# A fused attention and feed-forward kernel on one core: attention of batches 2 and 3 planned half a tile further ahead, pieces of the last tiles regrouped, and the fallback program moved within the instruction stream

## The chip, the core and the metric

The kernel runs on one core of a Trainium2 chip. The core has five engines with instruction streams of their own: PE (TensorE, matmuls), DVE (VectorE), ACT (ScalarE), POOL (GpSimd) and SP (SyncE, which here issues DMAs). [...] The metric is the device time of one execution in microseconds, lower is better.

## The reference

Attention over 4 batches, 8 heads, 768 positions and a head size of 64, where some heads ("retrieval" heads, flagged in an input; three of eight here) see all earlier positions, and the others see only the first `n_sink` = 4 positions and the last `window` = 64. Its output, as 3072 rows of 512, goes through a feed-forward layer with the activation h - tanh(h).

```python
def _attn_ref(q, k, v, is_retrieval, n_sink, window):
    scores = scale * np.matmul(q, k.transpose(0, 1, 3, 2))
    causal = rel >= 0
    stream_keep = causal & (is_sink | in_win)
    mask = np.where(retr[0, :, 0, 0, None, None], full_mask, stream_mask)
    scores = np.where(mask[None, :, :, :], scores, -1000000000.0)
    scores = scores - np.max(scores, axis=-1, keepdims=True)
    a = np.exp(scores)
    a = a / (np.sum(a, axis=-1, keepdims=True) + 1e-09)
    return np.matmul(a, v).astype(np.float32)

def _moe_ref(x, w_in, w_out):
    h = x @ w_in            # 512 -> 2048
    g = h - np.tanh(h)
    return (g @ w_out).astype(np.float32)   # 2048 -> 512
```

## The kernel before

**Tiles.** The 3072 rows are cut into 12 tiles of 256, three to a batch (tile t belongs to batch t // 3). For each tile there is attention (4 pairs of heads), a first layer of 8 units and a second layer. Tiles 3 to 11 use heads sorted by rank, so that the flagged heads come first; this is right for up to four flagged heads. If there are more, a second complete program, the redo program, computes everything again without that assumption. A count of flagged heads is loaded into a register of each engine near the end, and each engine compares it with 4 and branches.

**The operations.** For a pair of heads of a tile: SP or POOL loads q, k and v (L609), POOL gathers them by rank into fp16 (L654, L690) and builds helper tiles `vf` and `kc` (L709 to L729, L669, L679), SP transposes q and k with two DMA transposes a tile (L573, tile `QK`), PE computes scores (L1082), ACT the exponentials (L1095, tiles `pt` for pairs with flagged heads and `ptn` for the others), DVE multiplies with a mask (L1145, L1111, L1117; L1135 for tile 2), PE multiplies with the values (L1174), DVE divides by the sum (reciprocal L1194, scaling L1206 into `x16t`), and SP transposes the finished tile (L1238, tile `xT`). First layer: PE (L1298, 8 matmuls of 256 columns for a unit), ACT tanh (L1310), DVE the gate (L1317, tile `gt`, or `gu` for tile 2). Second layer: for tiles up to 7, 16 matmuls of 512 columns for each half of the tile (L1356), ACT evacuation (L1330), a store by SP.

**Tiles 8 to 11 have a cheaper second layer.** It uses seven products of half size in place of eight (the function `piece`, L1478, 8 matmuls of 256 columns each). For it DVE makes four sums of parts of w_out once for all tiles (`combine`, L1396: five steps in four parts each, called T below), and four sums of parts of the tile's gates for each tile (`sums`, L1446, called S, written into `m4`, in `SH` parts each). The results are put together by ACT (`take`, L1513), DVE (`fold`, L1532) and POOL (`add`, L1543) and stored by `send` (L1563). For tiles 8 to 10, `step(t, i)` runs beside unit i of the next tile's first layer and does what the table `STEPS` lists for i: numbers are pieces, letters are takes, folds and stores. For tile 11, `finale` does all seven pieces in one go.

**The order.** Every operation is recorded with an engine, a cost and what it reads and writes; the record's place is its priority. The class `Plan` then lays all of them out in time: at each step the engine that can start first takes its ready operation of the lowest priority number, with PSUM banks, buffers and DMA queues accounted for. The order that comes out is the order in which each engine's instructions are issued. The places in the record come from slots: one slot for each first-layer unit. `point(h)` is the slot of half tile h. The attention of batches 2 and 3 is cut into six visits a batch, each with three score units; visit i of batch b is recorded at half tile 6b - LEAD + i, its gather `GA` slots ahead, its loads `LD` slots ahead. `CUT1` does the like for the tiles of batch 1. `TWHEN` says over which slots the T sums are recorded (the first sixteen parts from the first entry to the second, the last four at the third); a part also reads a mark that the first gate of tile `TG` writes, if that gate is recorded before it.

**The end.** The last instructions of the main program are the last folds and stores. The last store is issued by ACT, the one before by SP. Then each engine compares and branches. The redo program stands directly behind that branch, so an execution that does not need it takes the branch, to a block of closing waits (SP waits there for all landings) and on to the common end with two barriers. A hint about this branch is given to each engine at the start of the program:

```python
tc.mark_branch_hint_location("redo", hint="LikelyTaken", engines=[...])
...
with tc.If(many[0] > NGEN, label="redo"):
    program(False)
```

Names and lines of the prediction's steps: scores L1082, exponentials L1095, masks L1145 and L1111, values L1174, first layer L1298, gates L1317, T sums L1396, S sums L1446, pieces L1478, folds L1532, stores L1563, transposes L573 (`QK`) and L1238 (`xT`), value loads L609 (`rawv`), the branch and the closing waits L1889, the hint and the common end L1921.

Of the kernel before, what the change touches and what calls it, by code (L numbers as in the profile page):

```python
# [255 lines left out]
def kernel(  # L256
# [14 lines left out]
    ALU = mybir.AluOpType  # L271
# [3 lines left out]
    DM = out.shape[1]  # L275
# [3 lines left out]
    NTT = NT // TT  # L279
# [8 lines left out]
    NGEN = H // 2  # L288
# [19 lines left out]
    Engine = mybir.EngineType  # L308
# [28 lines left out]
    CM = DM // 2  # L337
# [10 lines left out]
    many = []  # L348
# [6 lines left out]
    CASTS = (('ACT', 'DVE'), ('ACT', 'ACT'))  # L355
    CUT = (-4.5, -4.0, 5.25, 9.5)
    GATE = {3: (1, 0), 4: (1, 0)}
    CUT1 = (-8.0, -7.0, 3.0, 14.5)
    FLEX = 2
    ST = 8  # L360
    TQ = 4
    TG = 4
    SH = 2
    TWHEN = ((6, 0), (8, 0), (9, 1))
    STEPS = {1: (1, 4, "a"), 3: (2, 6, "e"), 5: (5, "b"), 7: (3, 7, "f")}
    TRI = ()
    SPLIT = 1 << 30
    LEAD = 3
    QUART = 7
    LD = 14  # L370
    GA = 10
    FROM = 3
    BR = 1
    AFTER = {3: 2}
# [12 lines left out]
    def program(first):  # L387
# [1004 lines left out]
        def combine(k, h, fn, a, b, w=lambda: ()):  # L1392
# [5 lines left out]
                ),  # L1398
                r=every + [("T", x, h) for x in range(1, 5) if x != k] + [("at", TG)],
                w=[("T", k, h), *w()], port=True,  # L1400
# [27 lines left out]
        def summed(k):  # L1428
            return [("S", k, h) for h in range(SH)]

        def sums(t):
# [4 lines left out]
            for k, fn, a, b, r in (  # L1436
# [4 lines left out]
            ):  # L1441
                for h in range(SH):
                    cs = slice(h * NC // SH, (h + 1) * NC // SH)
                    op(
                        "DVE", 90 + 690 // SH,
                        lambda k=k, fn=fn, a=a, b=b, cs=cs: getattr(nc.vector, fn)(  # L1446
                            out=S4[k][:, cs, :], in0=a()[:, cs, :], in1=b()[:, cs, :]
                        ),
                        r=g_[h * NFU // SH : (h + 1) * NFU // SH] + [("S", x, h) for x in r],
                        w=[("S", k, h)] + ([("m4", x) for x in range(HP)] if t == ST else []),  # L1450
# [5 lines left out]
        def piece(t, p, beside=None):  # L1456

            gt, ig, tag = gts[t]
            A = lambda i, f: lambda c: gt()[:, 2 * c + f, i * 128 : (i + 1) * 128]
            W = lambda f, m: lambda c: W_(f, m)[:, c, :]  # L1460
            T = lambda k: lambda c: T_(k)[:, c, :]
            S = lambda k: lambda c: S4[k - 1][:, c, :]
            lhs, rhs, r = {
                1: (A(0, 0), W(0, 0), []), 2: (A(0, 1), W(1, 0), []),
                3: (S(4), W(1, 1), summed(3)), 4: (A(1, 1), T(4), both(4)),
                5: (S(1), T(1), summed(0) + both(1)),
                6: (S(2), T(2), summed(1) + both(2)),
                7: (S(3), T(3), summed(2) + both(3)),
            }[p]
# [83 lines left out]
        def send(t, x, lo, hi, dst, ring="SP"):  # L1553

            ot, io = unit(t, x)
            how = "(r two) m -> r two m" if mixed(t) else "(two r) m -> r two m"
            rows = out[t * TT : (t + 1) * TT, :].rearrange(how, two=2)

            def go():
                src = ot()[:, lo:hi]  # L1560
                if len(dst(rows).shape) == 3:
                    src = src.rearrange("p (a b) -> p a b", b=dst(rows).shape[2])
                engs[ring].dma_start(out=dst(rows), in_=src)  # L1563

            dma(
                ring, 420, go, 128, (hi - lo) * 0.18, r=at_(t, x, lo, hi) + [("ot", io)], lag=(500, 800),
            )
# [3 lines left out]

        def step(t, i):

            for what in STEPS.get(i, ()):
                if what == "a":
                    take(t, 1, "A", 0, DM)
                elif what == "e":
                    fold(t, 2, "A", 0, "E", 0)
                elif what == "b":
                    take(t, 5, "A", 0, CM)  # L1580
                    add(t, "POOL", "tensor_sub", ("E", CM), ("A", 0), ("E", CM))
                    add(t, "POOL", "tensor_add", ("A", CM), ("A", 0), ("A", CM))
                elif what == "f":
                    fold(t, 3, "E", CM, "F", 0)
                    send(t, "F", 0, DM, columns(1))
                    add(t, "POOL", "tensor_sub", ("E", CM), ("A", CM), ("F", CM))
                    send(t, "E", 0, DM, columns(0))
                else:
                    piece(t, what, {4: 1, 6: 2, 7: 3}.get(what))

        def finale(t):

            piece(t, 1)
            take(t, 1, "A", 0, CM)
            piece(t, 4)
            take(t, 4, "F", 0, CM)
            piece(t, 2)
            fold(t, 2, "A", 0, "E", 0, CM)
            send(t, "E", 0, CM, lambda rows: rows[:, 0, 0:CM])
            piece(t, 6)  # L1600
            fold(t, 6, "A", 0, "E", CM, CM)
            add(t, "POOL", "tensor_add", ("F", 0), ("E", CM), ("F", 0))
            piece(t, 5)
            fold(t, 5, "E", CM, "A", CM, CM, 1.0, ALU.subtract)
            piece(t, 7)
            fold(t, 7, "F", 0, "F", 0, CM, -1.0)
            send(t, "F", 0, CM, lambda rows: rows[:, 1, 0:CM])
            fold(t, 7, "A", CM, "F", CM, CM)
            send(t, "F", CM, DM, lambda rows: rows[:, 1, CM:DM])
            piece(t, 3)  # L1610
            fold(t, 3, "A", CM, "E", CM, CM)
            send(t, "E", CM, DM, lambda rows: rows[:, 0, CM:DM], "ACT")
# [181 lines left out]
        if first and fast:  # L1794
            spread_over([by_rank], BR, BR)
            qs = quads()
            spread_over(qs[: 4 * TQ], slot_of[TWHEN[0]], slot_of[TWHEN[1]])
            spread_over(qs[4 * TQ :], slot_of[TWHEN[2]], slot_of[TWHEN[2]])
        spread_over(att_pairs(1) + [lambda: scale_v(1, SV)], 0, 0)
# [7 lines left out]
        for b in range(FLEX, NTT // NG) if first and fast else ():  # L1807
# [36 lines left out]
        for s, what in enumerate(slots):  # L1844
            if first and fast and s == point(2 * NG * FLEX - LEAD - 1):
                P.split = len(P.ops)
            fs = plan.get(s, [])
            mid = (len(fs) + 1) // 2
            for i, x in enumerate(what):
# [8 lines left out]
                else:  # L1858
                    t, ts, f0, f1, c0, c1 = x[1:]
# [3 lines left out]
        last = NTT - 1  # L1863
        if first and fast:

            def count():
                many.append(
                    nc.values_load(
                        count_i[0:1, 0:1], min_val=0, max_val=H,
                        skip_runtime_bounds_check_because="it counts the flags of H heads",  # L1870
                    )
                )
                tc.mark_branch_hint_location("redo", hint="LikelyTaken", engines=[Engine.Activation, Engine.PE, Engine.DVE, Engine.SP, Engine.Pool])

            op("SP", 500, count, r=["count", ("gt", gts[last][1], NFU - 1)])
        if quick(last):
            sums(last)
            finale(last)
        else:
            O_group(last, 0, 0, NFB)  # L1880
            O_group(last, 1, 0, NFB, 0, half, "DVE", "SP")
            O_group(last, 1, 0, NFB, half, DM, "ACT", "ACT")

        with tc.manual_schedule():
            P.run()

    program(True)
    if fast:
        with tc.If(many[0] > NGEN, label="redo"):  # L1889
            program(False)  # L1890


# [33 lines left out]
```

## Time and profile before

| | us |
|---|---|
| median of 3 runs | 230.2 |
| lowest and highest | 229.33, 230.72 |
| the profiled execution | 230.94 |
| its span in the profile | 229.2 |

The profile shows one execution. Its page lists busy time by engine, a picture of the span in 40 slices, the DMA queues, the chain of work that ended last, and the costliest groups of instructions; further views give groups by stage, one line's or one tile's instructions, and a timeline. A row of a timeline has start, length, engine, line, operation, tiles written and read, and how many such instructions are merged in it; "SPq" or "ACTq" is work of an engine's sequencer, such as issuing a DMA or branching. A matmul's shown length overlaps the next one's, so the distance between starts is what a matmul costs PE.

### The profile page before, as it was taken

The page shows a single profiled execution, that of the slowest core. Times are in us where ns is not written, and L with a number is a line of the kernel's source. Part 1 is how long each engine was busy: PE and PEld are TensorE (multiplying, and loading weights), DVE is VectorE, ACT ScalarE, POOL GpSimd, SP SyncE. Part 2 cuts the span into 40 slices and gives each one's busy share as a digit, 9 for nine tenths or more (in the row PEclk, how much of TensorE's full clock was granted, in tenths as well). Part 3 has the DMA queues.
Part 4 walks back from the last instruction along what each step waited for, and adds up shares of the span by engine and source line. Part 5 has one row for each costly group of instructions (what it writes and reads, how often), then busy time and mean ns, then how long its engine had stood idle before and what let it go on. Part 6 is the DMA issues. An engine that isn't in the chain of part 4 may idle for free.

```text
span 229.2 us, 6385 instructions
## 1 busy us (share of the span) xinstructions
PE 219.0 (96%) x2415; PEld 166.6 (73%) x2415; DVE 165.8 (72%) x401; ACT 141.1 (62%) x219; POOL 109.0 (48%) x241
## 2 busy tenths in 40 slices
PE   7979999999999999999999999999999999999990
PEld 7556687788986666765765867675868889898880
DVE  5787957865684955989886575476889599684891
ACT  3828839977466847746466657655883766732610
POOL 8989344775641918777465829290000021042020
PEclk9999999999999999999999999999999999999999
DMA  5999999999999999999999999936031042022032
GB/s 157 150 188 203 202 191 223 215 181 238 194 153 212 193 179 236 230 252 172 257 201 227 205 227 185 235 94 141 3 92 49 0 49 93 3 47 94 0 114 80
DMA packets 103877, 35.33 MB, mean 154 GB/s; under 512 B 90658, under 2 KB 101922, under 8 KB 103842
## 3 DMA queue, kind: packets, MB, share of 16 engines
q1 hardware_dynamic: 86544, 27.14, 57.8%
q0 software_dynamic: 17152, 7.60, 25.5%
q8 instruction: 20, 0.33, 0.6%
q10 hardware_dynamic: 146, 0.13, 0.2%
q14 instruction: 15, 0.12, 0.2%
HBM read 27.26 MB, written 6.29 MB: 146 GB/s over the span
## 4 chain that ended last, share of the span: by engine, by line
PE 71%; DMA 11%; POOL 6%; DVE 3%; ACT 3%; SPq 2%; issue 2%; POOLq 0%; DVEq 0%
PE banks L1298 29%; PE banks L1356 21%; PE banks L1478 10%; DMA win<-in_moe_w_in_dram 7%; PE banks L1174 6%; PE banks L1082 5%; DMA rawqk<-in_k_dram 2%; DMA QK<-t 2%; SPq L573 2%; POOL v L507 2%; ACT pt L1095 1%; POOL win L621 1%; POOL t L654 1%; POOL t16p L540 1%; DVE ot L1532 1%
## 5 line engine op out<-in xcount | busy, mean ns | idle before, releaser
L1298 PE MATMUL banks<-xT,win 128*128 128x256 f16 x768 | 94.8, 273 | 0.8 <-DVE gt L1317 0.6
L1298 PEld LDWEIGHTS <-win 128*128 128x128 f16 x768 | 73.0, 98 | 16.4 <-issue 1.6
L1310 ACT ACTIVATE th<-banks 128x512 f32<-128x512 f32 x96 | 57.2, 604 | 39.4 <-PE banks L1298 38.3
L1317 DVE SCALAR_TENSOR_TENSOR gt<-th,banks 128x512 f16<-128x512 f32 x88 | 59.7, 682 | 18.6 <-ACT th L1310 17.8
L1095 ACT ACTIVATE pt<-banks 128x768 f16<-128x768 f32 (+1 forms) x60 | 53.0, 922 | 10.5 <-PE banks L1082 10.2
L1356 PE MATMUL banks<-wout,gt 128*128 128x512 f16 (+1 forms) x288 | 57.1, 332 | 0.0
L654 POOL CAST t<-rawqk 128x256 f16 x72 | 29.2, 451 | 31.9 <-DMA rawqk<-in_k_dram 31.9
L1356 PEld LDWEIGHTS <-gt 128*128 128x128 f16 x288 | 25.8, 98 | 13.8 <-issue 1.0
L1543 POOL TENSOR_TENSOR ot<-gu,ot 128x256 f32<-128x256 f32 x6 | 4.5, 749 | 57.2 <-ACT gu L1513 42.5
L1206 DVE TENSOR_TENSOR x16t<-banks,rinv 128x128 f32 (+1 forms) x80 | 22.5, 286 | 1.1
L1082 PE MATMUL banks<-QK 64*128 64x128 f16 (+1 forms) x364 | 21.0, 238 | 1.0 <-DMA QK<-t 0.8
L690 POOL CAST v<-rawv 128x128 f16 x72 | 21.9, 349 | 0.0
L1082 PEld LDWEIGHTS <-QK 64*128 64x128 f16 x364 | 12.8, 94 | 10.0 <-issue 7.3
L1095 ACT ACTIVATE ptn<-banks 128x1024 f16<-128x1024 f32 (+1 forms) x18 | 17.1, 953 | 3.6 <-DVE x16t L1206 2.4
L1174 PEld LDWEIGHTS <-pt 128*128 128x128 f16 x420 | 15.9, 97 | 4.4 <-DVE pt L1145 0.9
L1174 PE MATMUL banks<-v,pt 128*128 128x65 f16 x220 | 16.5, 193 | 0.4 <-DVE xT L970 0.3
L1145 DVE TENSOR_TENSOR pt<-pt,m4r 128x1024 f16<-128x1024 f16 (+1 forms) x18 | 12.5, 696 | 5.1 <-ACT pt L1095 5.0
L1330 ACT ACTIVATE ot<-banks 128x512 f32<-128x512 f32 (+1 forms) x20 | 10.5, 524 | 8.5 <-PE banks L1356 7.2
L1117 DVE TENSOR_TENSOR ptn<-ptn,mS 128x1024 f16<-128x1024 f16 x12 | 9.6, 804 | 7.6 <-ACT ptn L1095 7.4
L1478 PEld LDWEIGHTS <-m 128*128 128x128 f16 x128 | 12.2, 98 | 1.7 <-issue 0.2
L1174 PE MATMUL banks<-vf,pt 128*128 128x65 f16 x200 | 13.1, 193 | 0.2 <-ACT pt L1095 0.2
L1194 DVE RECIPROCAL rinv<-banks 128x4 f32<-128x4 f32 x48 | 8.2, 175 | 5.5 <-PE banks L1174 5.0
(105 smaller groups left out, 239.9 us busy)
## 6 DMA issues: line engine op xcount, KB each, us to landing
rawqk<-in_q_dram SPq DMA_DIRECT2D x18, 256.0 KB, 4.2
rawqk<-in_k_dram SPq DMA_DIRECT2D x18, 256.0 KB, 4.6
out_dram<-ot SPq DMA_DIRECT2D x18, 256.0 KB, 2.6
rawv<-in_v_dram SPq DMA_DIRECT2D x16, 256.0 KB, 5.1
win<-in_moe_w_in_dram POOLq DMA_DIRECT2D x4, 512.0 KB, 11.7
wout<-in_moe_w_out_dram POOLq DMA_DIRECT2D x4, 512.0 KB, 13.3
out_dram<-ot SPq DMA_DIRECT2D x11, 128.0 KB, 4.0
v<-in_v_dram POOLq DMA_DIRECT2D x6, 128.0 KB, 9.5
```

Source lines behind the costliest of these rows:

```text
L654: nc.gpsimd.tensor_copy(out=c5()[:, :, :, s_ : s_ + 1, :], in_=r5()[:, :, :, at, :])
L690: nc.gpsimd.tensor_copy(out=v1s[b]()[:, g * NB : g * NB + NB, RANK[s_] : RANK[s_] + 1, 0:D], in_=rv()[:, :, at, :],)
L1082: nc.tensor.matmul(out=sc()[:, hh, o : o + nb * 128], lhsT=lhsT, rhs=QK[p_, hp, q_0 : q_0 + nb * 128], start=not added, stop=not added or ...
L1095: lambda pt=pt, sc=sc, gi=gi, wid=wid: nc.scalar.activation(out=pt()[:, :, 512 * gi : 512 * gi + wid], in_=sc()[:, :, 0:wid], func=AF.Exp, ...
L1145: nc.vector.tensor_mul(out=pv, in0=pv, in1=m)
L1174: nc.tensor.matmul(out=av()[:, i, hh, :], lhsT=pt()[:, hh, co : co + 128], rhs=vv, start=(jb == first_jb), stop=(jb == qb),)
L1206: nc.vector.tensor_mul(out=xt()[:, :, at, :], in0=av()[:, :, hh : hh + 1, 0:D], in1=rinv()[:, :, hh : hh + 1].unsqueeze(3).to_broadcast([1 ...
L1298: nc.tensor.matmul(out=ph()[:, j, :], lhsT=w_in_t[fb // 4][:, cb, f0 : f0 + 128], rhs=x, start=(cb == 0), stop=(cb == HP - 1),)
L1310: lambda: nc.scalar.activation(out=th()[:], in_=ph()[:], func=AF.Tanh, scale=1.0 / XS),
L1317: lambda: nc.vector.scalar_tensor_tensor(out=gt()[:, u * FU : (u + 1) * FU, :], in0=th()[:], scalar=-XS, in1=ph()[:], op0=ALU.mult, op1=AL ...
L1356: nc.tensor.matmul(out=po()[:, c0:c1], lhsT=gt()[:, f, ts * 128 : ts * 128 + 128], rhs=w_out_t[:, f, c0:c1], start=(f == 0), stop=(f == NF ...
L1478: nc.tensor.matmul(out=po()[:, at : at + CM], lhsT=lhs(c), rhs=rhs(c), start=c == 0, stop=c == NC - 1,)
```

## The change

It has five parts.

1. Attention of batches 2 and 3: `LEAD` from 3 to 4, so each visit is recorded one half tile earlier; `GA` from 10 to 7, so the gather comes 7 slots ahead of the visit instead of 10. `CUT1` shifts the attention of tiles 4 and 5 in the record.
2. T sums: the first sixteen parts are recorded from tile 4 on instead of tile 6 (`TWHEN`), the last four two slots later in tile 9; the mark that they read is tile 5's (`TG`).
3. Pieces: tiles 8 and 9 start their pieces at unit 2 instead of 1, tile 10 keeps the old table under the name `STEPL`. Each S sum is one instruction over the whole tile instead of two over its halves (`SH`), which makes 16 instructions of DVE fewer.
4. The old `finale` is kept as `finale_b`, and `FIN = 0` selects it; a new `finale` with another order of pieces stands in the file and is not called. The second-last store goes to ACT (`ENDS`).
5. The hint is gone, and the `If` gets `preferred_fallthrough_block=False`.

```diff
-    CUT1 = (-8.0, -7.0, 3.0, 14.5)
+    CUT1 = (-8.0, -5.0, 4.0, 14.5)
...
-    TG = 4
-    SH = 2
-    TWHEN = ((6, 0), (8, 0), (9, 1))
-    STEPS = {1: (1, 4, "a"), 3: (2, 6, "e"), 5: (5, "b"), 7: (3, 7, "f")}
+    TG = 5
+    SH = 1
+    TWHEN = ((4, 0), (8, 0), (9, 3))
+    STEPS = {2:(1, 4, "a"),4:( 2, 6, "e"), 5: (5, "b"), 7:(3, 7, "f")}
+    STEPL = {1: (1, 4, "a"), 3: (2, 6, "e"), 5: (5, "b"), 7: (3, 7, "f")}
...
-    LEAD = 3
+    LEAD = 4
+    FIN = 0
+    ENDS = "ACT"
...
-    GA = 10
+    GA = 7
...
-            for what in STEPS.get(i, ()):
+            for what in (STEPS if t < NTT - 2 else STEPL).get(i, ()):
...
         def finale(t):
...
+        def finale_b(t):
...
             fold(t, 7, "F", 0, "F", 0, CM, -1.0)
             send(t, "F", 0, CM, lambda rows: rows[:, 1, 0:CM])
             fold(t, 7, "A", CM, "F", CM, CM)
-            send(t, "F", CM, DM, lambda rows: rows[:, 1, CM:DM])
+            send(t, "F", CM, DM, lambda rows: rows[:, 1, CM:DM], ENDS)
             piece(t, 3)
             fold(t, 3, "A", CM, "E", CM, CM)
             send(t, "E", CM, DM, lambda rows: rows[:, 0, CM:DM], "ACT")
...
-                tc.mark_branch_hint_location("redo", hint="LikelyTaken", engines=[...])
...
-            finale(last)
+            (finale if FIN else finale_b)(last)
...
-        with tc.If(many[0] > NGEN, label="redo"):
+        with tc.If(many[0] > NGEN, label="redo", preferred_fallthrough_block=False):
             program(False)
```

In the built instruction streams the blocks stand in this order: before, main program, redo program, closing waits, common end; after, main program, closing waits, redo program, common end. So in both there is one jump over the redo program on each engine: before, it is the compare ahead of the closing waits; after, it is an unconditional branch behind them. On SP 117 instructions lie between branch and target in both, on the other engines between 114 (POOL) and some 4,870 (PE).

More of the change, by code (lines that the diff above doesn't have):

```diff
@@ L1596, in finale @@
             take(t, 4, "F", 0, CM)
+            piece(t, 6)
+            fold(t, 6, "A", 0, "E", CM, CM)
+            add(t, "POOL", "tensor_add", ("F", 0), ("E", CM), ("F", 0))
+            piece(t, 7)
+            fold(t, 7, "F", 0, "F", 0, CM, -1.0)
+            send(t, "F", 0, CM, lambda rows: rows[:, 1, 0:CM])
+            piece(t, 5)
+            fold(t, 5, "E", CM, "A", CM, CM, 1.0, ALU.subtract)
+            fold(t, 7, "A", CM, "F", CM, CM)
+            send(t, "F", CM, DM, lambda rows: rows[:, 1, CM:DM])
+            piece(t, 3)
+            fold(t, 3, "A", CM, "E", CM, CM)
+            send(t, "E", CM, DM, lambda rows: rows[:, 0, CM:DM], ENDS)
+            piece(t, 2)
+            fold(t, 2, "A", 0, "E", 0, CM)
+            send(t, "E", 0, CM, lambda rows: rows[:, 0, 0:CM], "ACT")
+        def finale_b(t):
+            piece(t, 1)
+            take(t, 1, "A", 0, CM)
+            piece(t, 4)
+            take(t, 4, "F", 0, CM)
             piece(t, 2)
@@ L1872, in count @@
                 )
-                tc.mark_branch_hint_location("redo", hint="LikelyTaken", engines=[Engine.Activation, Engine.PE, Engine.DVE, Engine.SP, Engine.Pool])
             op("SP", 500, count, r=["count", ("gt", gts[last][1], NFU - 1)])
```

## Prediction

> **What bounds the kernel now.** I read the page first, then the busy time by stage, then PE's own timeline where it is not full, then everything behind PE's last matmul.
>
> ```profile
> PE 219.0 (96%) x2415; PEld 166.6 (73%) x2415; DVE 165.8 (72%) x401; ACT 141.1 (62%) x219; POOL 109.0 (48%) x241
> ...
> PE 71%; DMA 11%; POOL 6%; DVE 3%; ACT 3%; SPq 2%; issue 2%; POOLq 0%; DVEq 0%
> ```
>
> PE is busy 96% of the span of 229.2 us and carries 71% of the chain that ended last. The table by stage (columns: stage, its length, then busy us of PE, PEld, DVE, ACT, POOL) tells where anything is left:
>
> ```profile
> 90.00:103.00 13.00, 13.00 (x140) 9.49 (x137) 11.45 (x29) 8.12 (x12) 10.43 (x25) 1.00 1.07 230
> 103.00:109.00 6.00, 5.80 (x61) 3.31 (x60) 5.75 (x15) 3.90 (x6) 4.54 (x11) 1.00 1.00 176
> 109.00:120.00 11.00, 11.00 (x105) 7.54 (x104) 9.49 (x24) 6.50 (x10) 6.82 (x18) 1.00 1.10 229
> 120.00:222.00 102.00, 102.00 (x1090) 79.56 (x1088) 75.25 (x169) 61.52 (x94) 29.60 (x70) 1.00 0.49 104
> ```
>
> From 120 to 222 us PE is busy 102.00 of 102.00 us at a granted clock of 1.00: an order that does the same matmuls cannot finish that stage sooner. The one hole behind 90 us lies in 103 to 109, where DVE is busy 5.75 of 6.00 us. PE's timeline there:
>
> ```profile
> 106.50 0.36 PE L1174 MATMUL banks<-v,pt 128*128 128x65 f16 x6
> 106.69 0.60 PE L1298 MATMUL banks<-xT,win 128*128 128x256 f16 x4
> 107.39 0.35 PE L1174 MATMUL banks<-v,ptn 128*128 128x65 f16 x6
> 107.58 0.60 PE L1298 MATMUL banks<-xT,win 128*128 128x256 f16 x4
> 108.28 0.35 PE L1174 MATMUL banks<-v,pt 128*128 128x65 f16 x6
> ```
>
> Two rows of the chain of waits give what a matmul occupies when nothing is late: 0.216 us with 512 columns, 0.109 with 256.
>
> ```profile
> 144.75 1.73 PE banks L1356 x8
> ...
> 210.31 6.99 PE banks L1298 x64
> ```
>
> Four of 256 columns take 0.44 us, so PE should go on at 107.13 and 108.02 but goes on at 107.39 and 108.28: two waits of 0.26 us, and one of 0.15 before 106.50, where eight of 512 columns from 104.61 should have ended at 106.34. Together 0.67 us. The chain says what was late:
>
> ```profile
> 105.00 0.55 DVE t16p L1396
> 105.54 0.89 DVE pt L1145
> 106.44 0.89 DVE ptn L1111
> 107.33 0.43 DVE t16p L1396
> 107.75 0.48 DVE pt L1145
> ```
>
> The masks of tile 6 queue on DVE behind the weight sums of line 1396. Everything after PE's last matmul is the other place:
>
> ```profile
> 223.88 0.42 DVE L1532 SCALAR_TENSOR_TENSOR ot<-banks,gu 128x256 f32<-128x256 f32 x1
> 224.00 0.51 SPq L1563 DMA_DIRECT2D out_dram<-ot  x1
> 224.34 0.39 ACTq L1563 DMA_DIRECT2D out_dram<-ot  x1
> ```
>
> ```profile
> L1889 SPq EVENT_SEMAPHORE  x8: 17/17/17, 225.1 to 227.5; - x8
> ...
> L1889 PEldq COMPARE_BRANCH  x1: 2091/2091/2091, 222.2 to 222.2; - x1
> ...
> L1889 SPq COMPARE_BRANCH  x1: 73/73/73, 224.6 to 224.6; - x1
> ```
>
> ```profile
> L1921 SPq EVENT_SEMAPHORE  x14: 17/28/28, 227.6 to 229.1; - x14
> ...
> L1921 SPq BRANCH_PREFETCH_HINT  x1: 56/56/56, 0.8 to 0.8; - x1
> ```
>
> The last fold ends at 224.30, ScalarE issues the last store at 224.34, SP has waited for its landing by 227.5, and closing waits and barriers take to 229.2. SP's branch over the redo program (224.6) lies ahead of that wait, so it is hidden under 2.9 us of landing.
>
> **The change part by part.**
>
> *Attention ahead (LEAD 4, GA 7, CUT1, TWHEN, TG).* The same 2,415 matmuls stand in the built order, the first 1,025 (to 90.8 us) in the same places. The first score visit of tile 6 moves from place 1,157 (104.0 us) to 1,115 (97.8 us). Loads and gathers hardly move: GpSimd's list differs by one memset, SP's by small swaps. Of the weight sums, five now stand on DVE ahead of the mask at 50.31, the other eleven of the first sixteen behind tile 5's first gate, that is behind 109; so none is left in 94 to 109, where they took some 6 us.
>
> ```profile
> L1396 DVE TENSOR_TENSOR t<-wout x4: 389/536/826, 94.2 to 98.1; 128x512 f16<-128x512 f16 x4
> ```
>
> ```profile
> 50.31 1.39 DVE L1135 SCALAR_TENSOR_TENSOR pt<-m,pt 128x512 f16<-128x512 f16 x2 [1.72 <-ACT pt L1095]
> ```
>
> ```profile
> 53.43 0.25 PE L1174 MATMUL banks<-vf,pt 128*128 128x65 f16 x3
> ```
>
> Five at 0.39 to 0.54 us take 2.0 to 2.7 us from 48.6 us, of which 1.72 is idle now: the mask starts 0.3 to 1.0 late and ends by 52.7 at the latest, before PE wants it at 53.43. Cost nothing; without that cover, up to 1.0. Queued behind are a reciprocal and two scalings whose bank PE wants later.
>
> The 0.67 us go if tile 6's masks now find DVE free. The built order has 8 + 4 matmuls of the layers between the scores and their first use (0.44 + 0.86 + 0.87 = 2.2 us) where it had 1.7. Full gain -0.67. What is late next is tile 7:
>
> ```profile
> 99.18 1.93 SPq L609 DMA_DIRECT2D rawv<-in_v_dram  x1
> 101.66 2.06 SPq L1238 DMA_TRANSPOSE xT<-x16t  x1
> 103.83 2.62 SPq L573 DMA_TRANSPOSE QK<-t  x2
> ```
>
> ```profile
> 109.35 0.59 PE L1356 MATMUL banks<-wout,gt 128*128 128x512 f16 x2
> ```
>
> Its score visit takes the place that PE now reaches at 109.35, about 108.6 with the waits gone. Its operands come from the two transposes, the second issued at 105.1; from issue to landing they need
>
> ```profile
> DMA to landing us min/median/max: 3.2/3.3/5.0
> ```
>
> that is 108.3 or later. In the new order SP issues xT of tile 5 before that value load; if xT's scalings come about a us sooner with the weight sums gone, all lands about 107.5. While SP waits for them, the value load and both transposes queue behind it. New waits: between 0 and 1.5 us (the longest landing, 5.0, gives 110.1); I take +0.25, near the low end, for the median is the likelier landing and the next visit that needs new operands, tile 8's, stands 160 places further on. The other DMAs that move past each other on SP are stores and loads that no one awaits within a us.
>
> *Last tile's first layer (STEPL, later STEPS) and whole-tile sums (SH 1).* The first layer of tile 11 moves from places 2,291 to 2,354 in one run to 2,239 to 2,342 between the pieces of tile 10. PE has no hole there to fill, so 0. Whole sums wait for a whole tile: four of at most 2 x 0.42 us follow the last gate, which now ends about 217.3 instead of
>
> ```profile
> 218.03 0.68 DVE L1317 SCALAR_TENSOR_TENSOR gt<-th,banks 128x512 f16<-128x512 f32 x1
> ...
> 221.10 0.41 DVE L1446 TENSOR_TENSOR m<-gt,m 128x512 f16<-128x512 f16 x1
> ```
>
> 217.3 + 3.4 + one fold of 0.68 = 221.4, against 222.81 less 0.7, when the last piece starts. Hidden, by 0.7 us; without the earlier layer it would cost about 0.7.
>
> *Second-last store by ScalarE (ENDS; FIN 0 keeps the old finale under a new name).* It is ready at 223.88 and can be issued at 223.91 instead of 224.00; only the last store queues behind its 0.39 us and is ready at 224.30. Between -0.1 and +0.4; taken with the landing, next.
>
> *Redo program behind the end, no hint.* The hint at 0.8 us leaves every engine: -0.06. In the built order the redo program now stands behind the closing waits but ahead of the common end. So each engine falls through its compare and, after its closing waits, takes a jump over the redo program without a hint. For SP this jump comes after the last landing, with nothing over it. Its price: SP's branch starts at 224.6 and the next wait at 225.1, 0.5 us for a jump over 117 instructions, and the new one spans 117 too: +0.5. Bounds 0.07 (its own row) and 2.1 (PE's row, much of which is waiting for its matmuls); I take 0.5, the same engine and distance. [...] PE, VectorE and ScalarE jump from about 224.4 to 225.0; even 2.1 us later they stand before the barrier that SP reaches at 228.4.
>
> ```profile
> q8 instruction: 1, 0.02, 1.4%
> ```
>
> ```profile
> q10 hardware_dynamic: 18, 0.02, 3.9%
> ```
>
> The first row is the DMA table of 224.0 to 229.2: one code packet of 16 KB takes 1.4% of 16 engines' 5.2 us, 1.16 us on one engine. The second is that of 226.0 to 227.2: the last store's queue moves 18 of its 144 packets there, about one engine's share of two late rows, after all others are done by 226. If code no longer lies ahead of them the landing comes 1.0 sooner; if two packets do, up to 0.6 later. I take -0.2.
>
> *Sum*, on the span: -0.06 - 0.67 + 0.25 + 0.5 - 0.2 = -0.18, 229.0. The profiled execution took 230.94 around a span of 229.2 (1.74 outside) and stands 0.74 above the median of 230.2, so I forecast 230.0.
>
> **The rivals.**
>
> A, slower: the jump finds its code missing on SP. [...] Here: SP's unhinted jump at about 227 costs PE's 2.1 us in place of 0.5, or more: 230.0 + 1.6 = 231.6. It decides the time as soon as SP's jump exceeds about 1.9. For it: no hint is left, and code packets do run at the end. Against: 117 instructions are few and SP's present jump of that length takes 0.5. Chance 0.17.
>
> B, slower: tile 7's transposes land after 5.0 us, SP being held by xT of tile 5 (+1.5 instead of 0.25), and the eleven sums, now behind 109, queue one of 0.5 us ahead of a mask: 231.7. For it: four sums stand in 109 to 120 now, eleven then. Against: DVE has 1.5 of 11 us free there, and gates can wait where masks cannot. Chance 0.10.
>
> C, faster: the final stores come clear of code packets (-1.0 instead of -0.2) with no new wait: 229.0. For it: the 18 late packets. Against: PE's unhinted jump fetches code at about the same time. Chance 0.23.
>
> D, the change does not do what it says: the stall only moves, and the jump is dearer by what the branch was: 230.0 + 0.5 = 230.5. This stays with the forecast's side, chance 0.12; the forecast itself 0.38.
>
> **How the numbers follow.** A change within 0.5% (1.15 us) is about what a measurement of this kernel can tell from none. Forecast and D: same, 0.50. C: faster, 0.23. A and B: slower, 0.27. The forecast's own range is 229.1 to 230.9; with A's fetch of up to 2 us and C's gain it becomes 228.6 to 231.9.
>
> **What would show it.** Right: no hole in PE between 103 and 112; tile 6's scores near 97.8; the last fold near 223.6; no hint row; SP's branch row after its last landing wait, and about 0.5 us to its next row. Wrong: PE waiting for the QK transposes near 108.5, holes behind 120, a branch row on SP of 2 us, or a last store that lands 2 us after issue instead of 3.1. Two or more such waits that I did not list would put it beyond the range.

## The result and the profile after

The changed kernel takes 231.84 us (median of 11 runs, 230.78 to 232.20) against 230.66 us before (median of 11, 229.33 to 231.87): a ratio of 1.0052, 95% interval 1.0030 to 1.0073. The forecast was 230.0 us and no change. The time lies outside the forecast's own range, 229.1 to 230.9, and just inside the wider one, 228.6 to 231.9, whose upper end came from rival A. The change costs about 1.2 us, more than the measurement's uncertainty.

The profiled execution took 232.18 us around a span of 230.0 us. From its page, the engine totals and the chain that ended last:

```profile
PE 218.7 (95%) x2415; PEld 167.1 (73%) x2415; DVE 161.4 (70%) x385; ACT 141.2 (61%) x219; POOL 109.4 (48%) x241
...
PE 86%; DMA 3%; ACT 3%; POOL 2%; DVE 2%; issue 1%; POOLq 0%
```

PE carries still more of the chain (86%, before 71%). The table by stage (stage, length, then busy us of PE, PEld, DVE, ACT, POOL, then granted clock):

```profile
90.00:97.00 7.00, 6.47 (x80) 4.73 (x78) 4.92 (x11) 5.69 (x9) 4.18 (x8) 1.00 1.08 211
97.00:103.00 6.00, 5.98 (x73) 4.36 (x73) 4.80 (x15) 3.37 (x6) 5.64 (x16) 1.00 0.99 190
103.00:109.00 6.00, 6.00 (x52) 3.91 (x50) 4.01 (x11) 3.00 (x6) 2.81 (x7) 1.00 1.10 226
109.00:120.00 11.00, 11.00 (x118) 7.49 (x113) 10.12 (x25) 8.20 (x12) 7.12 (x18) 1.00 1.02 206
120.00:222.00 102.00, 102.00 (x1073) 79.69 (x1071) 72.42 (x154) 59.29 (x92) 30.85 (x71) 1.00 0.44 102
```

The hole between 103 and 109 us is gone (6.00 of 6.00, before 5.80), and VectorE is busy 4.01 us there instead of 5.75. But 90 to 97 us, which was full (7.00), now has a hole (6.47). The timeline there (start, length, engine, line, operation; in brackets the idle time before and what ended it):

```profile
94.62 0.69 DVE L1120 TENSOR_TENSOR ptn<-ptn,mS 128x1024 f16<-128x1024 f16 x1 [0.94 <-ACT ptn L1098]
...
95.45 1.03 PE L1359 MATMUL banks<-wout,gt 128*128 128x512 f16 x4
95.65 0.60 ACT L1313 ACTIVATE th<-banks 128x512 f32<-128x512 f32 x1 [0.57 <-PE banks L1301]
...
96.28 0.69 DVE L1320 SCALAR_TENSOR_TENSOR gt<-th,banks 128x512 f16<-128x512 f32 x1 [0.28 <-ACT th L1313]
...
97.02 0.19 PE L1177 MATMUL banks<-vf,ptn 128*128 128x65 f16 x1 [0.54 <-DVE gt L1320]
```

Four matmuls of 512 columns from 95.45 are through at 96.31 (4 x 0.216 us, what one took in the profile before: 8 in 1.73 us), and PE goes on at 97.02: 0.71 us. The mask of line 1120 was done at 95.31, so it is not the mask. PE waits for a gate of line 1320 (96.28 to 96.97), which itself comes behind an activation.

The end, first the timeline behind the last matmul:

```profile
222.58 0.89 DVE L1535 SCALAR_TENSOR_TENSOR ot<-banks,gu 128x256 f32<-128x256 f32 x2
222.69 0.34 SPq L1566 DMA_DIRECT2D out_dram<-ot  x1
223.02 0.87 ACTq L1566 DMA_DIRECT2D out_dram<-ot  x2
```

then the rows of line 1914 (the branch and the closing waits) and of line 1946 (the end; after the count: shortest/median/longest ns, then first and last start):

```profile
L1914 SPq EVENT_SEMAPHORE  x8: 17/17/17, 223.2 to 227.8; - x8
...
L1914 PEldq COMPARE_BRANCH  x2: 95/2256/4418, 221.4 to 223.2; - x2
...
L1914 SPq COMPARE_BRANCH  x2: 38/46/53, 223.1 to 227.9; - x2
L1914 ACTq COMPARE_BRANCH  x2: 38/46/53, 223.9 to 224.1; - x2
```

```profile
L1946 SPq EVENT_SEMAPHORE  x14: 17/28/28, 228.4 to 230.0; - x14
...
L1946 DVEq DRAIN  x2: 10/36/61, 226.9 to 229.5; - x2
L1946 ACTq DRAIN  x2: 8/38/67, 227.2 to 229.5; - x2
L1946 PEldq DRAIN  x2: 8/40/73, 227.7 to 229.5; - x2
```

and the DMA queues between 224.1 and 227.7 us (packets, MB, share of 16 engines' time):

```profile
q10 hardware_dynamic: 244, 0.22, 19.4%
q8 instruction: 1, 0.02, 3.7%
q14 instruction: 3, 0.02, 2.6%
```

How these read: the last fold ends at 223.47, 0.83 us sooner than in the profile before (224.30), and ScalarE issues the last store at about 223.50 (the second of the two from 223.02). Before, SP had seen the last landing by 227.5, some 3.1 us after that issue at 224.34; now it sees it by 227.8, some 4.3 us after the issue. SP's jump then goes out at 227.9 and its next wait starts at 228.4: 0.5 us, with nothing beside it. PE's jump takes 4.4 us (223.2 to 227.6), and ScalarE's and VectorE's next instructions come at 227.2 and 226.9, about 3 us after their jumps. All three stand before the barrier in time. But the one 16 KB code packet of queue q8 has taken 3.7% of 16 x 3.6 us, or 2.1 us; before, it took 1.16 us. The trace doesn't name the engine whose code a packet carries. Queue q8 is taken for PE's here, since its 21 packets of 16 KB are 0.34 of the 0.48 MB of code in the span of this profile and 4,830 of the 6,367 instructions are PE's matmuls and weight loads; q14, with 18 packets of 8 KB, is taken for the other engines'.

The span grows by 0.83 us between the two profiles, from 229.21 to 230.03. PE reaches its matmul number 1,000 (counted from 0) 0.84 us sooner, at 88.60 instead of 89.44 us. From there to the start of its last matmul it takes 134.13 us in both. Behind that start it takes 7.30 us instead of 5.63. So the earlier last fold isn't the work of the closed hole: it comes from the stretch ahead of matmul 1,000, which holds the same matmuls in the same order. Other runs of the kernel before's order reach that matmul anywhere from 87.5 to 89.4 us.

Two things outside these rows. The time outside the span is 2.10 us on average in the changed kernel's 11 runs, against 1.74 us in the profiled execution of before; later runs of before average 1.75. So about 0.35 of the 1.2 us lies there. And this profile has a slow stretch of TensorE's clock at 16 to 20 us (0.61 granted). One of six later profiles with this order has such a stretch too (0.69), and in all seven PE reaches matmul 1,000 at 87.8 to 88.6 us, so it isn't what costs.

### The profile page after: what moved, and what is told of

Its sections match the earlier page's. It is cut to its first block, busy times and chain, and to the rows that moved or that the text cites. A ratio compares the mean times of both kernels' runs of the same rounds, so it can differ in the third digit from the quotient of the medians.

```text
span 230.0 us, 6367 instructions
## 1 busy us (share of the span) xinstructions
PE 218.7 (95%) x2415; PEld 167.1 (73%) x2415; DVE 161.4 (70%) x385; ACT 141.2 (61%) x219; POOL 109.4 (48%) x241
## 4 chain that ended last, share of the span: by engine, by line
PE 86%; DMA 3%; ACT 3%; POOL 2%; DVE 2%; issue 1%; POOLq 0%
PE banks L1301 35%; PE banks L1359 24%; PE banks L1481 11%; PE banks L1085 7%; PE banks L1177 7%; DMA t16p<-in_k_dram 3%; ACT pt L1098 1%; PE banks L1074 1%; POOL v L510 1%; ACT QK L971 1%; ACT th L1313 1%; DVE gt L1320 1%; PE banks L990 0%; POOL A L758 0%; PE banks L1259 0%
## 5 line engine op out<-in xcount | busy, mean ns | idle before, releaser
L1301 PE MATMUL banks<-xT,win 128*128 128x256 f16 x768 | 97.4, 274 | 0.5 <-DVE gt L1320 0.5
L657 POOL CAST t<-rawqk 128x256 f16 x72 | 31.6, 486 | 36.4 <-DMA rawqk<-in_k_dram 33.4
L1546 POOL TENSOR_TENSOR ot<-gu,ot 128x256 f32<-128x256 f32 x6 | 5.3, 883 | 54.7 <-ACT gu L1516 45.9
L693 POOL CAST v<-rawv 128x128 f16 x72 | 18.8, 307 | 0.0
L1120 DVE TENSOR_TENSOR ptn<-ptn,mS 128x1024 f16<-128x1024 f16 x12 | 8.8, 736 | 9.1 <-ACT ptn L1098 9.0
```

The costliest lines, as they stand in the source:

```text
L657: nc.gpsimd.tensor_copy(out=c5()[:, :, :, s_ : s_ + 1, :], in_=r5()[:, :, :, at, :])
L693: nc.gpsimd.tensor_copy(out=v1s[b]()[:, g * NB : g * NB + NB, RANK[s_] : RANK[s_] + 1, 0:D], in_=rv()[:, :, at, :],)
L1301: nc.tensor.matmul(out=ph()[:, j, :], lhsT=w_in_t[fb // 4][:, cb, f0 : f0 + 128], rhs=x, start=(cb == 0), stop=(cb == HP - 1),)
```

## The experiments

Twelve kernels ran. Names that begin with a_ start from the changed kernel, with b_ from the kernel before. All ratios are to the kernel before, run beside them, with the 95% interval. A first table, since all the sections draw on it. "Order": attention as before or new. "Redo": ahead of the closing waits (old) or behind them (new). PE from 1,000 is the time from the start of PE's matmul number 1,000, counted from 0, to that of its last, in the profiled run; there is one profile of each kernel. The next columns are us after the start of the last matmul: PE's last 16 KB code packet that starts between 1 us ahead of that matmul and 3 us behind it (start + length), the last landing as seen by SP, the end of the span. In the five runs with the old place and no hint one more such packet starts at 3.27 to 3.65 us, just ahead of the landing.

| run | order | redo | hint | ratio | PE from 1,000 | code packet | landing | end |
|---|---|---|---|---|---|---|---|---|
| before | old | old | yes | 1 | 134.13 | 1.39 + 1.15 | 3.86 | 5.63 |
| after | new | new | no | 1.0052 [1.0030, 1.0073] | 134.13 | 1.46 + 2.11 | 4.99 | 7.30 |
| a_oldbranch | new | old | yes | 1.0030 [1.0010, 1.0051] | 134.13 | 1.07 + 1.49 | 4.40 | 6.17 |
| b_newbranch | old | new | no | 1.0037 [1.0016, 1.0059] | 133.51 | 1.46 + 2.30 | 5.20 | 7.50 |
| b_nohint | old | old | no | 0.9982 [0.9960, 1.0003] | 133.93 | -0.37 + 1.44 | 3.65 | 5.42 |
| a_endsSP | new | new | no | 1.0061 [1.0037, 1.0086] | 134.12 | 1.50 + 1.50 | 4.61 | 6.93 |
| b_same | old | old | yes | 0.9998 [0.9980, 1.0015] | 133.84 | 1.43 + 1.17 | 4.12 | 5.90 |
| a_nohint_oldlayout | new | old | no | 0.9998 [0.9980, 1.0016] | 134.13 | -0.26 + 1.66 | 3.67 | 5.69 |
| b_attention | new | old | yes | 1.0022 [1.0002, 1.0042] | 134.13 | 1.28 + 1.33 | 4.13 | 5.91 |
| b_layers | old | old | yes | 0.9990 [0.9971, 1.0008] | 134.32 | 0.62 + 1.05 | 3.51 | 5.28 |
| a_noredo | new | none | no | 0.9907 [0.9876, 0.9939] | 134.12 | none | 2.55 | 3.56 |
| b_nohint_layers | old | old | no | 0.9970 [0.9946, 0.9995] | 133.52 | -0.28 + 1.55 | 3.78 | 5.56 |
| a_nohint_cut1old | new, CUT1 old | old | no | 0.9996 [0.9978, 1.0014] | 134.64 | -0.26 + 1.33 | 3.58 | 5.36 |
| b_nohint_layers_weights | old, sums new | old | no | 0.9959 [0.9931, 0.9988] | 133.42 | -0.26 + 1.70 | 3.81 | 5.58 |

### Undoing the branch alone, or doing it alone

a_oldbranch is the changed kernel with:

```diff
+                tc.mark_branch_hint_location("redo", hint="LikelyTaken", engines=[Engine.Activation, Engine.PE, Engine.DVE, Engine.SP, Engine.Pool])
...
-        with tc.If(many[0] > NGEN, label="redo", preferred_fallthrough_block=False):
+        with tc.If(many[0] > NGEN, label="redo"):
```

> The changed kernel with only the branch part taken back: the hint is there again and the redo program lies ahead of the closing waits again. Theory T (the redo program's new place and the missing hint cost about 2 us behind the last matmul: the last landing 1.1 us later against its issue, SP's jump 0.5 us, 0.4 us outside the span): about 0.8 us below the kernel before, a ratio of 0.996, with a last store that lands about 3.1 us after its issue and 1.7 us outside the span. Rival S (the reordered schedule loses it, for instance by PE's half clock between 16 and 20 us): still about 1.2 us above, 1.005. Rival E (two stores on ScalarE's queue land late): the landing stays at 4.2 us after its issue, and the time is about 0.3 us above.

b_newbranch is the kernel before with the same two lines the other way round.

> The kernel before with only the branch part of the change: no hint, the redo program behind the closing waits. Theory T: about 2.0 us above the kernel before, 1.009, with misses of 3 to 4 us at the jumps of PE, VectorE and ScalarE and more time outside the span. Rivals S and E: within 0.5 us of it, 1.000 to 1.002 (SP's jump of 0.5 us alone).

a_oldbranch measured 1.0030, between theory T (0.996) and S (1.005). T is outside the interval and S at its edge, but S alone leaves out the end: the tail, the time from the start of the last matmul to the end of the span, falls from 7.30 to 6.17 us, so the branch is worth about 1.1 us there. Rival E's landing of 4.2 us behind the issue did not come either (3.6 us, 4.40 less 0.77). Still, that is later than T's 3.1, and something in the new order costs too. b_newbranch measured 1.0037, less than T's 1.009; the rivals' 1.002 lies inside its interval, but its tail has what T named. Its rows of line 1888, the branch:

```profile
L1888 SPq EVENT_SEMAPHORE  x8: 17/17/17, 222.7 to 226.9; - x8
...
L1888 PEldq COMPARE_BRANCH  x2: 95/2364/4633, 220.4 to 222.1; - x2
...
L1888 SPq COMPARE_BRANCH  x2: 38/46/53, 222.5 to 227.0; - x2
```

PE's jump is long (4.6 us) in the old order too, and SP's jump again stands behind the landing. The tail grows from 5.63 to 7.50 us: 1.34 us of it is the landing (3.86 to 5.20), 0.5 us the jump. This edit changes hint and place together.

### The hint or the place

b_nohint takes only the hint away:

```diff
-                tc.mark_branch_hint_location("redo", hint="LikelyTaken", engines=[Engine.Activation, Engine.PE, Engine.DVE, Engine.SP, Engine.Pool])
```

> The kernel before without the hint, the redo program where it was, so that the branch over it is taken without a hint ahead of the last landing's wait. If the missing hint is the cost (T1): the engines' branches miss as in the changed kernel (3 to 4 us on PE), the landing is late, 1.0 to 1.5 us above, about 1.005. If the place is the cost (T2: the same jump, behind the closing waits instead of under them): within 0.3 us, 1.000.

a_nohint_oldlayout is the changed kernel with only the place put back:

```diff
-        with tc.If(many[0] > NGEN, label="redo", preferred_fallthrough_block=False):
+        with tc.If(many[0] > NGEN, label="redo"):
```

> The changed kernel with the redo program back in its old place but still without the hint. If the new place of the redo program is the cost and the missing hint is not (theory P): the tail behind PE's last matmul is 5.4 to 6.2 us as in the two other kernels with the old place, against 6.9 to 7.5 with the new one, and the time is at or below that of the changed kernel with the old branch, 0.999 to 1.003. If the missing hint costs (rival): the tail is 6.9 us or more, 1.005.

0.9982 and 0.9998: the missing hint costs nothing. It seems to help: 0.18% between before and b_nohint, 0.32% between a_oldbranch and a_nohint_oldlayout, 0.20% between b_layers and b_nohint_layers further down. No pair settles it alone, for each ratio's interval reaches about 0.2% to either side, but all three point the same way. The place is the cost: from b_nohint to b_newbranch it is 1.0037 - 0.9982 = 0.0055, from a_nohint_oldlayout to the changed kernel 1.0052 - 0.9998 = 0.0054. That is about 1.25 us in both orders, and the landing alone comes 1.55 us (3.65 to 5.20) and 1.32 us (3.67 to 4.99) later. The rows of b_nohint's branch show how a long jump can cost so little:

```profile
L1888 SPq EVENT_SEMAPHORE  x8: 17/17/17, 223.5 to 225.2; - x8
...
L1888 PEldq COMPARE_BRANCH  x1: 3912/3912/3912, 220.0 to 220.0; - x1
```

PE's branch takes 3.9 us here as well. But it starts 1.4 us ahead of the start of PE's last matmul (PE's queue runs ahead), so its code packet starts at -0.37 us and is through at 1.07, when the last store, issued at 0.77 us, has not begun to move (its packets start behind 1.5 us). In the new place PE first falls through, waits for its last matmuls, and only then jumps, at 0.46 us. The packet then starts at 1.46, in the middle of the last stores. The 8 KB code packets of the other engines lie among the stores in both places (starts at 1.2 to 3.0 us), so they don't make the difference.

What the stores wait for can be read from the packets themselves. In b_newbranch PE's packet ends at 3.76 us behind the start of the last matmul. From 224.6 to 225.3 us (2.9 to 3.6 behind it) no packet of any queue starts. From 225.4 to 226.5 us there are only these:

```profile
q1 hardware_dynamic: 9, 0.01, 4.0%
q10 hardware_dynamic: 9, 0.01, 2.1%
```

A store has 128 rows of 1 KB, and q1 carries SP's, q10 ScalarE's. So 8 rows of each of the last two stores, a sixteenth, and one packet of 4 bytes each are left when all other rows have moved, and they go one after another from 3.75 to 4.71 us. In the changed kernel it is the same: 16 rows of q10, from 3.56 to 4.51 us, behind a code packet that ends at 3.57. In each of the seven runs whose code packet ends behind 2.5 us, a row of a store starts within 0.02 us of that end. The trace doesn't name the DMA engine of a packet, but one sixteenth of each store queuing behind the code packet is what one shared engine of the 16 would give. In the table the landing follows the packet's end by 1.3 to 1.8 us wherever that end lies behind 2.5 us, and stands at 3.5 to 3.8 us where it is earlier.

### The second-last store's queue

```diff
-    ENDS = "ACT"
+    ENDS = "SP"
```

> The changed kernel with only the second-last store given back to SP. Theory T: within 0.3 us of the changed kernel, about 1.005 against the kernel before. Rival E (the last store lands late because two stores share ScalarE's queue): the last landing comes 1 us sooner against its issue, about 1.000 to 1.001.

1.0061: the store's queue is not what makes the landing late. Its landing at 4.61 goes with a code packet of 1.50 us in place of 2.11.

### No branch at all

```diff
-    if fast:
-        with tc.If(many[0] > NGEN, label="redo", preferred_fallthrough_block=False):
-            program(False)
```

> The changed kernel without the redo program and without its branch; it leaves out the fallback for inputs with more marked heads than the fast program holds, and the main program is the same. Theory P (the loss behind the last matmul is the unhinted jump: its code fetches lie ahead of the last stores on one DMA engine, and SP's own jump comes after the landing): the last landing is seen 3.6 to 4.0 us after the last matmul instead of 5.0, the tail is 5.0 to 5.7 us instead of 7.3, and the ratio is about 1.000, at most 1.001. Rival (the stores or the reordered last tiles make the landing late): landing at 4.5 us or later, tail 6.5 us, 1.003.

The fallback is left out here, so this is no version to use; it says what the branch costs at all. 0.9907, far below the 1.000 expected. Its stores and its end (line 1943 is the end in this kernel), and the DMA queues in the 3.6 us from 223.7:

```profile
222.58 0.86 ACTq L1566 DMA_DIRECT2D out_dram<-ot  x2
```

```profile
L1943 SPq DRAIN  x3: 7/7/13, 225.0 to 225.3; - x3
...
L1943 PEldq DRAIN  x2: 13/824/1635, 221.0 to 225.3; - x2
```

```profile
q10 hardware_dynamic: 221, 0.19, 16.2%
q14 instruction: 1, 0.01, 0.5%
```

No q8 row is left. The last store, issued at about 223.05, has landed before SP's drain at 225.0, less than 2 us later, where the changed kernel needs 4.2 and the kernel before 3.1. PE's matmuls end in the same order (134.12 us from matmul 1,000), so the 3.7 us between the tails, 7.30 and 3.56, are the branch, its code and the closing waits that go with it: 2.4 us of landing (4.99 to 2.55), 0.5 us of SP's jump, and 0.8 us of closing waits, most of which SP here gets through ahead of the landing. Even the kernel before pays about 2 us of this. No run moves PE's packet alone.

### Attention and layers apart

b_attention is the kernel before with five constants of the change:

```diff
-    CUT1 = (-8.0, -7.0, 3.0, 14.5)
+    CUT1 = (-8.0, -5.0, 4.0, 14.5)
-    TG = 4
+    TG = 5
-    TWHEN = ((6, 0), (8, 0), (9, 1))
+    TWHEN = ((4, 0), (8, 0), (9, 3))
-    LEAD = 3
+    LEAD = 4
-    GA = 10
+    GA = 7
```

> The kernel before with the scheduling constants of attention and weight sums alone (CUT1, TG, TWHEN, LEAD, GA). Theory H (the new order makes PE wait at 96 us for VectorE, 0.54 us in each of the three runs that have it, and the holes at 103 to 109 us that it removes are there in only some runs): 0.3 to 0.7 us above, 1.001 to 1.003, with the wait at 96 us in the trace. Rival (the loss of the new order lies in the last tiles): 0.5 us or more below, 0.998 or less, without that wait.

b_layers is the kernel before with SH 1, the new STEPS for tiles 8 and 9, and STEPL for tile 10:

```diff
-    SH = 2
-    STEPS = {1: (1, 4, "a"), 3: (2, 6, "e"), 5: (5, "b"), 7: (3, 7, "f")}
+    SH = 1
+    STEPS = {2:(1, 4, "a"),4:( 2, 6, "e"), 5: (5, "b"), 7:(3, 7, "f")}
+    STEPL = {1: (1, 4, "a"), 3: (2, 6, "e"), 5: (5, "b"), 7: (3, 7, "f")}
...
-            for what in STEPS.get(i, ()):
+            for what in (STEPS if t < NTT - 2 else STEPL).get(i, ()):
```

> The kernel before with the whole-tile sums and the last tile's steps alone (SH, STEPS, STEPL). Theory H: no hole arises behind 120 us and none goes, 1.000 with 0.001 to either side. Rival (the loss of the new order lies in the last tiles): 0.5 us above, 1.002 or more.

Theory H held in both: 1.0022, clear of 1 by little, and 0.9990. b_attention has the wait at 96 us:

```profile
96.95 0.19 PE L1174 MATMUL banks<-vf,ptn 128*128 128x65 f16 x1 [0.54 <-DVE gt L1317]
```

The column "PE from 1,000" says what the new order does to PE. All six runs of it take 134.12 or 134.13 us, to a hundredth. With the old order's attention the same matmuls took 133.42 to 134.32 us, differently in each execution. Measured from the shortest, the new order traded holes of 0 to 0.9 us that come and go for one of 0.7 us that was there each time.

### Taking the wait at 96 us away

a_nohint_cut1old, from a_nohint_oldlayout:

```diff
-    CUT1 = (-8.0, -5.0, 4.0, 14.5)
+    CUT1 = (-8.0, -7.0, 3.0, 14.5)
```

> The changed kernel with the redo program in its old place, no hint, and CUT1 as before. The built order then puts the matmuls of tile 5's second probabilities between and behind others, without the wait on VectorE that stands ahead of them in the changed kernel. Theory H (the wait of 0.54 us at 96 us is what the new order costs): no wait there, 0.5 us below the run a_nohint_oldlayout, a ratio of 0.9975. Rival (the wait only moves): a hole of 0.4 us or more elsewhere between 90 and 115 us, 1.000.

0.9996, not the 0.9975 of theory H: as the rival has it, the wait only moves. PE now stops for the same gates behind tile 5's probabilities instead of ahead of them, and again at 144 us:

```profile
96.65 1.03 PE L1301 MATMUL banks<-xT,win 128*128 128x256 f16 x8 [0.30 <-DVE gt L1320]
```

```profile
144.33 1.02 PE L1359 MATMUL banks<-wout,gt 128*128 128x512 f16 x4 [0.36 <-DVE gt L1320]
```

At 96 us PE stands still for 0.46 us (its last matmul of 65 columns before the hole starts at 96.16 and takes about 0.03, for such matmuls start 0.03 us apart from 96.07 to 96.16). From matmul 1,000 it takes 134.64 us, more than with the wait.

### Putting the good parts together

b_nohint_layers is b_nohint with the edit of b_layers.

> The kernel before without the hint and with the whole-tile sums and the last tile's steps of the change (SH, STEPS, STEPL). If the parts add up: -0.56 us and -0.12 us, a ratio of 0.997. If the gain of b_nohint was chance: 0.999 to 1.000.

b_nohint_layers_weights adds:

```diff
-    TG = 4
+    TG = 5
...
-    TWHEN = ((6, 0), (8, 0), (9, 1))
+    TWHEN = ((4, 0), (8, 0), (9, 3))
```

> As b_nohint_layers, and with the weight sums' times of the change (TG, TWHEN). The holes between 103 and 109 us were 0.67 us in the first profile of the kernel before and 0 to 0.28 us in three later ones with the same order, so their removal is worth 0.2 us at most: 0.996 to 0.997. Rival (the forecast's price of them, 0.67 us): 0.994.

0.9970 and 0.9959, both as the sums of parts had it; the rival's 0.994 lies inside the second interval too, so that price isn't excluded by the time. The second, 229.29 us against 230.10 us of the kernel before beside it, beats both kernels: no hint, the redo program where it was, the whole-tile sums and later steps, and the weight sums at their new times. Moving the weight sums alone, with LEAD, GA and CUT1 left as they were, leaves no wait at 96 us in its profile, and PE takes 133.42 us from matmul 1,000. That is the least of all, but only 0.1 us below b_newbranch and b_nohint_layers, and the 0.0011 between the two ratios is less than their uncertainty: what the weight sums give by themselves is not settled.

### The control

b_same is the kernel before, unchanged.

> A control: the kernel before, unchanged, sent as if it were a change. 1.000. So far the time outside the span was 1.76 us in the kernel before and 1.96 to 2.10 in every changed one; if it is about 1.97 here too, some 0.2 us (0.0009) of each ratio belongs to the comparison and not to the kernels.

0.9998, and 1.73 us outside the span. The kernel against itself shows no difference, so the 2.1 us outside the span in the changed kernel belong to it. They are not the branch's alone: 1.91 us in b_layers, which has branch and hint as before, 2.22 us in a_noredo, which has none, and 1.74 to 1.76 us in b_attention and b_nohint_layers. What makes them stays open.

## Why the prediction was wrong, point by point

*The last landing: this step failed.* The prediction took -0.2 us, with bounds of -1.0 and +0.6; the runs show +1.1 to +1.55. Its reading was that PE, VectorE and ScalarE could jump late at no cost, since "even 2.1 us later they stand before the barrier that SP reaches at 228.4". They do stand before the barrier, at 226.9 to 227.7. But the cost of their jumps isn't at the barrier. PE's code moves as a 16 KB packet (2.11 us) at the same time as the last stores, and the landing comes 1.1 us later in this pair of profiles (3.86 to 4.99 us behind the start of the last matmul), 1.32 and 1.55 us later when the place alone is changed. PE's jump took 4.4 us where the prediction allowed the 2.1 us of the old branch row, and instead of the two packets that its upper bound feared, one packet took nearly twice as long. The thought was there: against rival C the prediction says that "PE's unhinted jump fetches code at about the same time". But the sum gave it no price, and put the landing sooner instead of later. Falling through first puts PE's jump behind its last matmul (0.46 us after its start), where the old branch ran ahead of it (1.4 us).

*SP's jump, +0.5.* Right: 227.9 to 228.4 us, and 0.5 us in each run with the new place. The jump's own row in the trace is only 38 ns long, and yet the next instruction comes 0.5 us later, so the lower bound of 0.07, taken from the length of SP's row, is not what the jump costs here.

*The holes at 103 to 109 us, -0.67, and new waits, +0.25.* The holes went. But they had been read from one execution: the order of before spread over 0.6 us between four profiles (133.51 to 134.13), and moving the weight sums by themselves gave 0.0011, within the uncertainty. The new wait is 0.7 us, not 0.25, and stands at 96 us behind a gate, not at 108.5 behind tile 7's transposes. Against the profile of before the two cancel exactly (134.13 and 134.13 us); against its runs the new order costs 0.22% (b_attention, interval 0.02 to 0.42%). Two of the signs named in advance came true by luck: the last fold at 223.47 us (named: 223.6) and tile 6's scores at 97.8, which stand behind the new wait, owe it to a first stretch that was 0.84 us shorter in this profile, not to the closed hole.

*First layer, whole-tile sums, ENDS: 0.* Right within the measurement: 0.9990 for the first two, and 1.0061 against 1.0052 for giving the store back. The store was counted with the landing.

*The hint, -0.06.* Probably too small: its removal goes with 0.18 to 0.32% (0.4 to 0.7 us) in three pairs of runs, none of them clearly outside the noise alone. With the hint PE's code packet falls at 0.6 to 1.4 us behind the last matmul in the old place, without it at -0.3.

*The time outside the span* was taken as fixed at 1.74 us and is 2.10; its cause stays open.

*The rivals.* A's time (231.6) came near by luck, not by its mechanism: SP's jump, over 117 instructions, is through in 0.5 us, as before. The long jump is PE's: it takes 4.4 us, 0.46 to 4.88 us behind the start of the last matmul, and the 16 KB code packet moves within it, from 1.46 to 3.57. ScalarE and VectorE come to their next instruction about 3 us after their jumps. That the code itself was missing is a reading of these times; no run shows it apart. B did not happen: there is no wait at 108 to 109 us, and PE is busy 11.00 of 11.00 us from 109 to 120. C is the opposite of what happened. D was right in one half: the stall in PE's stream did only move.

In sum, by the runs: place +1.25 us, hint -0.4 to -0.7, attention +0.5, layers and store together between -0.4 and 0. That adds up to between +0.65 and +1.35, and +1.2 was measured; each of these parts is itself uncertain by some 0.5 us.

## What to carry to other kernels

Here the branch near the end cost by when its code was fetched (a packet from 1.46 us behind the start of the last matmul with the new place, from about -0.3 with the old one and no hint, and the landing 1.32 to 1.55 us later), not by how long PE stood at it (4.4 and 4.6 us with the new place, 3.9 in b_nohint): look for code packets between the last store's issue and its landing, and prefer an order in which the long engine's branch runs ahead of its last work. A transfer or a hole that one profile shows should be priced by how often it comes: the time between two fixed matmuls, over several profiles, tells a steady wait (134.12 or 134.13, six times) from a chance one (133.4 to 134.3). Where a big edit has parts that can be run apart, run them apart: here the parts that seem to gain (no hint, the whole-tile sums) were kept from showing by the place of the redo program, which costs more.

## What the hardware showed that was not expected

- With no branch and no code to fetch at the end, the last store is seen landed 1.8 us after its issue (2.55 against 0.77 us behind the last matmul); with code packets about, the same store takes 2.7 to 4.4 us (landings at 3.51 to 5.20).
- PE's 16 KB code packet of the table takes 1.05 to 1.7 us when it starts by 0.6 us behind the start of the last matmul, and 1.15 to 2.3 us when it starts at 1.1 to 1.5 us, among the last stores. Where it ends behind 2.5 us (seven runs), the last rows of the last stores move only from that end on.
- A branch hint 220 us ahead of its branch did not make the end sooner, and seems to make it later: with the redo program in its old place the landing is at 4.00 us with it (mean of five profiles, 3.51 to 4.40) and at 3.70 us without (mean of five, 3.58 to 3.81). The two ranges overlap.
